# Pairing heads two apart so that a weight piece's rows are neighbours, loading queries ahead of keys, and a new order of the first four chunks

## The chip, the cores and the metric

The kernel runs on one core of a Trainium2 chip. The metric is device time in microseconds (us) for one execution: the median over the runs shown. A core has a matrix engine (TensorE, PE in the profile, with its weight loads as PEld), VectorE (DVE), ScalarE (ACT), GpSimd (POOL) and SyncE (SP). SP, ACT and POOL also issue transfers, which sixteen DMA engines carry out. SBUF is the memory of 128 partitions that the engines work on, PSUM the memory that TensorE writes.

## The reference

Inputs are q, k and v (4 batches, 8 heads, 768 positions, 64 values a head, float32) and two weight matrices of float64, 512 x 2048 and 2048 x 512, which reach the kernel as 64-bit words.

```python
# attention (retention): gamma differs from head to head
for t in range(S):
    state = gamma * state + outer(k[t], v[t])
    y[t] = scale * q[t] @ state
x = y.transpose(0, 2, 1, 3).reshape(B * S, H * D)      # 3072 x 512
# then a gated layer
h = x @ w_in                                           # 3072 x 2048
sp = softplus(h)
out = (h * erf(sp)) @ w_out                            # 3072 x 512
```

## The kernel before, in words

The sequence of each batch is cut into chunks of 128 positions, six to a batch, 24 in all; chunk j is `j % 6` of batch `j // 6`. Two neighbouring chunks make a group of 256 tokens, which is the unit of the gated layer (`GT = 256`, 12 groups).

Within a chunk the recurrence is done as matrix products: the keys and the scaled queries are transposed (`ret_transpose`, T), scores are their product (`ret_scores`, S_), VectorE masks them with a triangle into a tile `am` (`ret_mask`, M), and the output is masked scores times V plus queries times the running state (`ret_out`, O_). `ret_out` also forms the chunk's own keys-times-values sum, which `ret_add` (A) adds to the state. `scale_q` (Q_) and `scale_v` (V_) multiply queries and values by per-head powers of the decay, which stand in `kq_s`.

Heads are handled in pairs, because two heads of 64 values fill the 128 partitions: pair `u` holds heads `2u` and `2u+1`. The output goes into a tile `xT` (`XC`) whose 128 partitions times four column groups are the 512 input features of the layer. In the kernel before, partition half `r` and group `g` hold head `4r + g`, so a group joins features that lie 256 rows apart in `w_in`.

The weights `w_in` come in eight pieces of 256 columns (1 MB of 64-bit words each). `load_piece` loads a piece into a tile `raw`, in transfers of 64 partitions. VectorE and ScalarE then convert the words to float32 (`conversion`, lines 184 to 210: five VectorE operations and one on ScalarE), and pieces 0 to 3 are converted in two halves. The generator `weight_steps` emits one step of it at a time: `next(weight_steps)` emits one, and `need("in", n)` emits until feature tile n is ready. Finishing a piece releases its `raw` tile and issues the load of the piece four further on; after pieces 0 and 1 also q, k and v of chunks 4 and 5 are loaded.

The order of work in the first stage is written out by hand. Loads are all issued on SP's queue, in the order k and q of a chunk, then v of the chunk before, with the first weight piece near the end. The calls below `T(0, 0)` fix the order on each engine, and `keep_warm` puts matmuls on the identity between them. The work of an engine runs strictly in that order. When the chunks 0 to 3 are done, `hidden_of` multiplies feature tiles of the weights with groups 0 and 1 (PE line 591), sixteen feature tiles in turn. Each result is copied by ScalarE into a tile `h` and stored to `HID` in device memory by two transfers on POOL's queue (line 601). The tiles `h`, and the small `am` of later chunks, share a ring of six buffers (`b2`). At feature tile 1, `load_block_scales` puts further transfers on POOL's queue: the row scale `by_b` (line 328) and sixteen small transfers into `kq_b` (line 332). The work of chunks 4 and 5 is spread over feature tiles 5 to 13 by the table `during`; `states` (lines 513, 524) makes their masked scores and states.

After that come ten groups in which TensorE multiplies with weights split into three parts (`unit`, line 616) while the remaining chunks are prepared, and then the last stage, which applies softplus and erf and multiplies with `w_out` (`project`, line 801).

Each transfer has a completion semaphore. SP and POOL each take theirs from eight in turn, and a transfer waits for the one that used its semaphore eight transfers earlier on that queue.

Of the kernel before, what the change touches and what calls it, by code (L numbers as in the profile page):

```python
# [21 lines left out]
P = 128  # L22
C = 128
JPC = 4
GT = 256


PAIRS = (0, 2, 1, 3)

BELOW = 1023 - 127  # L30

# [10 lines left out]
def kernel(  # L42
# [51 lines left out]
    KNP, VP = {}, {}  # L94

    def of_chunk(x, j):

        b, c = divmod(j, NC)
        return x[b, :, c * C : (c + 1) * C, :].rearrange("h p d -> p h d")

    def load(j):

        kq = b4("kq", [2, H, D])
        KN[j], QN[j] = kq[:, 0], kq[:, 1]
        for to, src in ((KN[j], k), (QN[j], q)):
            nc.sync.dma_start(to, of_chunk(src, j))  # L106

    def load_values(j):
        if j % 2 == 0:
# [4 lines left out]
    def load_pair(j):  # L114

        b, c = divmod(j, NC)
        KNP[j] = b4("kn", [2, H, D])
        KB[j], QB[j] = (b4(name, [HP, 2 * C]) for name in ("kb", "qb"))
        for s, d in itertools.product(range(2), range(2)):
            part = slice((2 * s + d) * 32, (2 * s + d + 1) * 32)  # L120
            for to, src in ((KB[j], k), (QB[j], q)):
                for u in range(HP):
                    nc.sync.dma_start(
                        to[part, u].rearrange("p (a d) -> p a d", d=32),
                        src[b, 2 * u + s, c * C : (c + 2) * C, d * 32 : (d + 1) * 32].rearrange(
                            "(a p) d -> p a d", p=32
                        ),
                    )
                yield
        for i in range(2):  # L130
            load_values(j + i)
        for i in range(2):
            KN[j + i] = KNP[j][:, i]
            nc.sync.dma_start(KN[j + i], of_chunk(k, j + i))
        yield

# [22 lines left out]

    def load_quarter(i):  # L160
# [140 lines left out]
    unscale = 1.0 / math.sqrt(D)  # L301

    def query_scale(c):
        nc.vector.reciprocal(kq_s[:, c, 1], kq_s[:, c, 0])
# [15 lines left out]
    def other_scales():  # L320
        query_scale(slice(2, NC))
# [3 lines left out]
    by_b = const.tile([P, 2, HP], F32, name="by_b")  # L325

    def load_block_scales():
        nc.gpsimd.dma_start(by_b[:, 1], decay_s)
        for s, d in itertools.product(range(2), range(2)):
            part = slice((2 * s + d) * 32, (2 * s + d + 1) * 32)  # L330
            for u in range(HP):
                nc.gpsimd.dma_start(
                    kq_b[part, 0, u, 0],
                    decay_k[:, 2 * u + s : 2 * u + s + 1].rearrange("(a p) h -> p (a h)", p=32),
                )

    def block_scales():
# [46 lines left out]
    def ret_transpose(j, part=None, names=None):  # L384
        for i, (x, store) in enumerate(((KN[j], KT), (QN[j], QT))):
            if part not in (None, i):
                continue
            p = ps_o.tile([P, HP, C], F32, name=names[i]) if names else ret_psum(ps_h if i else ps_r)
            for u in range(HP):
                nc.tensor.transpose(  # L390
                    p[:, u, :], x[:, 2 * u : 2 * u + 2, :].rearrange("p h d -> p (h d)"), ident
                )
            if i == 0:
# [23 lines left out]
    def ret_out(j, between=None, state_last=False):  # L417
# [21 lines left out]
            between()  # L439
        for h in (0, 4, 1, 5, 2, 6, 3, 7):  # L440
            nc.tensor.matmul(
                place(h), V[j][:, h, :], AM[j][:, h % 2, h // 2, :],
                start=(not c and h % 4 < 2), stop=True, skip_group_check=True,
            )

        new = SU[j] = pp[0][:, 2:, :].rearrange("p a (b d) -> p (a b) d", d=D)
        for h in range(H):
            r = h % 2
            nc.tensor.matmul(
                new[r * D : (r + 1) * D, h // 2, :], KN[j][:, h, :], V[j][:, h, :],  # L450
                start=False, stop=True, skip_group_check=True,
            )
        for r in range(2):
# [37 lines left out]
    def begin(j, pool=ps_h):  # L491

        SC[j] = [ret_psum(pool) for _ in range(2)]
        for hp in range(HP):
            for a, s in itertools.product(range(2), range(2)):
                t, own = slice(a * D, (a + 1) * D), slice(s * D, (s + 1) * D)
                nc.tensor.matmul(  # L497
                    SC[j][s][t, hp, :D], KT[j][own, hp, t], QT[j][own, hp, t], start=True, stop=True,
                )
        for u in range(HP):  # L500
            for r in range(2):
                for a in additions(j):
                    t, h = slice(a * D, (a + 1) * D), 2 * u + r
                    nc.tensor.matmul(  # L504
                        SC[j][a][r * D : (r + 1) * D, u, D:], KN[j][t, h, :], V[j][t, h, :],
                        start=True, stop=True,
                    )

# [17 lines left out]
    def results(j, names=None, pool=ps_r):  # L526
# [20 lines left out]
        for crossed in range(2):  # L547
            for u in PAIRS:
                for a in range(2):
# [2 lines left out]
                    own = slice(col * D, (col + 1) * D)  # L552
                    nc.tensor.matmul(  # L553
                        pp[a][own, 2 + u % 2, :D] if crossed else pp[a][own, u % 2, t],
                        V[j][t, 2 * u + r, :],
                        AM[j][t, r, u],
                        start=False, stop=True, skip_group_check=True,
                    )
# [416 lines left out]
```

## Time and profile before

| | |
|---|---|
| runs | 627.85, 628.66, 631.52 us, median 628.66 |
| profiled execution | 630.29 us, span 628.6 us |
| TensorE busy | 617.5 us (98%) |
| VectorE, ScalarE, GpSimd busy | 472.9, 346.8, 99.8 us |
| granted TensorE clock | 0.999 |

The profile is one execution. "Span" is the time from the first to the last recorded instruction; the execution takes slightly longer. In rows of the timeline the first number is the start, the second the duration, and what stands in brackets is the idle time of the engine ahead of it and what ended that. SPq, POOLq and the like are an engine's queue of instructions. "L591" is line 591 of the kernel before. The DMA rows give mean rates over all sixteen DMA engines.

### The profile page before, as it was taken

What the parts mean: (1) busy time and instruction counts of PE and PEld (TensorE: products, weight loads), DVE (VectorE), ACT (ScalarE), POOL (GpSimd) and SP (SyncE); (2) the same over time, 40 slices, a digit from 0 to 9 for tenths busy, and PEclk for the clock granted to TensorE, in tenths of its full rate; (3) what the DMA queues carried; (4) which work ended last, traced back from release to release, by engine and by line L of the source; (5) the groups of instructions that cost most, each with busy time, mean ns of one, the idle gap of its engine ahead of it and who ended that gap; (6) DMA issues with size and microseconds to landing.
All of it is one profiled execution on the core that took longest, in us unless ns stands there. A gap on an engine that the chain in (4) does not pass through costs nothing.

```text
span 628.6 us, 14668 instructions
## 1 busy us (share of the span) xinstructions
PE 617.5 (98%) x6080; PEld 555.9 (88%) x6080; DVE 472.9 (75%) x608; ACT 346.8 (55%) x430; POOL 99.8 (16%) x189
## 2 busy tenths in 40 slices
PE   8899999999999999999999999999999999999997
PEld 7688789999999999999999978888888888888886
DVE  4887899849598887878777997867676686768650
ACT  3333353322323333232349779898889889888920
POOL 1054442222322413222111110000000000000000
PEclk9999999999999999999999999999999999999999
DMA  9999888986859898787945751453334314432300
GB/s 190 209 217 213 227 211 192 244 224 150 242 142 262 207 237 227 214 219 190 271 165 167 261 170 70 136 168 101 115 119 168 129 43 162 139 94 103 101 33 34
DMA packets 165426, 106.37 MB, mean 169 GB/s; under 512 B 139632, under 2 KB 143984, under 8 KB 165360
## 3 DMA queue, kind: packets, MB, share of 16 engines
q1 hardware_dynamic: 152608, 67.53, 44.4%
q0 software_dynamic: 12192, 37.77, 17.7%
q8 instruction: 47, 0.77, 0.5%
q10 hardware_dynamic: 560, 0.14, 0.1%
q14 instruction: 19, 0.16, 0.1%
HBM read 69.75 MB, written 35.65 MB: 168 GB/s over the span
## 4 chain that ended last, share of the span: by engine, by line
PE 89%; DMA 6%; SPq 2%; DVE 1%; issue 1%; POOL 1%; ACT 0%; DVEq 0%; POOLq 0%
PE o L616 35%; PE o L801 21%; PE hp L801 10%; PE r L801 10%; PE hp L591 4%; DMA hid<-h 3%; DMA kq_b<-decay_k_dram 2%; SPq L106 1%; DMA v<-in_v_dram 1%; PE hp L497 1%; PE hp L616 1%; PE r L616 1%; PE r L542 1%; DMA raw<-in_moe_w_in_dram 1%; PE hp L504 1%; PE r L553 1%
## 5 line engine op out<-in xcount | busy, mean ns | idle before, releaser
L616 PE MATMUL o<-x_hi,w_hi 128*128 128x256 f32 x600 | 149.6, 287 | 0.0
L616 PE MATMUL o<-x_lo,w_lo 128*128 128x256 f32 x600 | 147.2, 283 | 0.6 <-issue 0.6
L616 PEld LDWEIGHTS o<-x_hi,w_hi 128*128 128x128 f32 x600 | 115.0, 192 | 2.1 <-issue 0.7
L263 ACT ACTIVATE h<-o 128x512 f32<-128x512 f32 x75 | 44.7, 596 | 127.9 <-PE o L616 127.1
L616 PEld LDWEIGHTS o<-x_lo,w_lo 128*128 128x128 f32 x600 | 115.1, 192 | 0.1
L756 DVE TENSOR_TENSOR e<-hid,e 128x1024 f32<-128x1024 f32 x48 | 56.6, 1222 | 58.2 <-ACT e L746 58.2
L616 PE MATMUL o<-x_dif,w_dif 128*128 128x256 f32 x600 | 84.1, 283 | 0.0
L639 POOL DMA_DIRECT2D hid<-h x80 | 44.6, 558 | 206.7 <-DVE h L264 204.3
L616 PEld LDWEIGHTS o<-x_dif,w_dif 128*128 128x128 f32 x600 | 77.4, 192 | 0.0
L801 PE MATMUL o<-w_dif,g_dif 128*128 128x512 f32 x192 | 73.7, 389 | 0.0
L264 DVE SCALAR_TENSOR_TENSOR h<-o,h 128x512 f32<-128x512 f32 x75 | 51.2, 683 | 25.5 <-ACT h L263 13.1
L801 PE MATMUL o<-w_lo,g_lo 128*128 128x512 f32 x168 | 65.4, 389 | 0.0
L801 PE MATMUL o<-w_hi,g_hi 128*128 128x512 f32 x168 | 65.4, 389 | 0.0
L257 DVE SCALAR_TENSOR_TENSOR g_dif<-g_hi,g_lo 128x1024 fp32r<-128x1024 f32 x48 | 58.8, 1225 | 3.2
L255 ACT ACTIVATE g_hi<-e 128x1024 fp32r<-128x1024 f32 x48 | 51.0, 1063 | 17.8 <-DVE e L756 15.1
L256 DVE TENSOR_TENSOR g_lo<-e,g_hi 128x1024 fp32r<-128x1024 f32 x48 | 58.6, 1222 | 0.2
L591 PE MATMUL hp<-xT,w 128*128 128x256 f32 x256 | 56.9, 381 | 1.6 <-DVE w L210 1.6
L591 PEld LDWEIGHTS hp<-xT,w 128*128 128x128 f32 x256 | 48.1, 190 | 8.3 <-issue 1.2
L746 ACT ACTIVATE e<-e 128x1024 f32<-128x1024 f32 x48 | 48.2, 1053 | 0.3
L742 ACT ACTIVATE e<-hid 128x1024 f32<-128x1024 f32 x48 | 48.2, 1052 | 0.3
L801 PEld LDWEIGHTS o<-w_dif,g_dif 128*128 128x128 f32 x192 | 36.0, 188 | 7.5
L801 PE MATMUL hp<-w_dif,g_dif 128*128 128x512 f32 x96 | 37.5, 390 | 0.6 <-DVE h L264 0.6
(166 smaller groups left out, 1069.9 us busy)
## 6 DMA issues: line engine op xcount, KB each, us to landing
hid<-hid SPq DMA_DIRECT2D x48, 512.0 KB, 4.8
hid<-h POOLq DMA_DIRECT2D x80, 256.0 KB, 3.6
raw<-in_moe_w_out_dram POOLq DMA_DIRECT2D x32, 256.0 KB, 5.1
v<-in_v_dram SPq DMA_DIRECT2D x24, 256.0 KB, 5.7
out_dram<-y SPq DMA_DIRECT2D x23, 256.0 KB, 2.1
kb<-in_k_dram SPq DMA_DIRECT2D x144, 32.0 KB, 3.2
qb<-in_q_dram SPq DMA_DIRECT2D x144, 32.0 KB, 3.0
kn<-in_k_dram SPq DMA_DIRECT2D x18, 256.0 KB, 6.7
```

The costliest lines, as they stand in the source:

```text
L255: nc.scalar.activation(hi, x, AF.Copy, scale=KEEP)
L256: nc.vector.tensor_tensor(lo, x, hi.bitcast(F32), op=ALU.subtract)
L257: nc.vector.scalar_tensor_tensor(dif, hi.bitcast(F32), Z, lo.bitcast(F32), op0=ALU.mult, op1=ALU.subtract)
L263: nc.scalar.activation(to, a, AF.Copy, scale=1 + 1 / Z)
L264: nc.vector.scalar_tensor_tensor(to, b, -1 / Z, to, op0=ALU.mult, op1=ALU.add)
L591: nc.tensor.matmul(HP_[ft][:, g], w[:, kk, ft % 2 * P : (ft % 2 + 1) * P], XC[g][:, kk], start=(kk == 0), stop=(kk == n_k - 1),)
L616: nc.tensor.matmul(to[:, u], W[n][i][:, kk * 2 * P + u * P : kk * 2 * P + (u + 1) * P], X[g][i][:, kk], start=(u == 0 and kk == 0 and i == ...
L639: nc.gpsimd.dma_start(HID[g][:, 2 * n : 2 * n + 2], h)
L742: nc.scalar.activation(E[n], HID_[n], AF.Softplus)
L746: nc.scalar.activation(E[n], E[n], AF.Erf)
L756: nc.vector.tensor_tensor(E[n], HID_.pop(n), E[n], op=ALU.mult)
L801: nc.tensor.matmul(Y[g][t][x // 2], G[n][x][:, f, t * P : (t + 1) * P], W_OUT[ft // 2][x][:, ft % 2 * d_model : (ft % 2 + 1) * d_model], s ...
```

## The change

A function gives the new pairing, for all chunks:

```diff
+def head(u, r):
+    return u // 2 + u % 2 * 4 + 2 * r
```

So the pairs are heads (0, 2), (4, 6), (1, 3), (5, 7). Every place that used `2 * u + r` for a head of V, K or a scale now uses `head`. Partition half `r` and group `g` of `xT` now hold head `2g + r`, which is the order of the rows of `w_in`. The first six chunks hold their queries and keys in the order of the pairs in SBUF, which takes two transfers each:

```diff
-        for to, src in ((KN[j], k), (QN[j], q)):
-            nc.sync.dma_start(to, of_chunk(src, j))
+        for to, src in ((QN[j], q), (KN[j], k)):
+            for c in range(2):
+                nc.sync.dma_start(to[:, c * HP : (c + 1) * HP], of_chunk(src, j)[:, c::2])
+        SLOT[j] = lambda u, r: 2 * u + r
```

A weight piece is loaded by two transfers of 128 partitions (piece 0 by two for each half):

```diff
-    def load_piece(n, *parts):
+    def load_piece(n, part=None):
...
-        rows = (slice(2), slice(2, 4)) if n == 0 else (slice(4),)
-        for part, g, r in itertools.product(parts or (None,), rows, range(2)):
-            f = slice(2 * P) if part is None else slice(part * P, (part + 1) * P)
+        f = slice(2 * P) if part is None else slice(part * P, (part + 1) * P)
+        for g in range(0, n_k, 2):
             nc.sync.dma_start(
-                RAW[n][r * D : (r + 1) * D].rearrange("p (g f) -> p g f", g=n_k)[:, g, f],
-                w_in[r * DH : (r + 1) * DH, n * 2 * P : (n + 1) * 2 * P].rearrange(
-                    "(g p) f -> p g f", p=D
-                )[:, g, f],
+                RAW[n].rearrange("p (g f) -> p g f", g=n_k)[:, g : g + 2, f],
+                w_in[g * P : (g + 2) * P, n * 2 * P : (n + 1) * 2 * P].rearrange(
+                    "(g p) f -> p g f", p=P
+                )[:, :, f],
             )
```

The order of the loads at the start:

```diff
     for j in range(1, JPC):
         load(j)
-        load_values(j - 1)
+        if j < JPC - 1:
+            load_values(j - 1)
     load_piece(0, 0)
+    load_values(JPC - 2)
+    load_piece(0, 1)
     load_values(JPC - 1)
-    load_piece(0, 1)
     for n in range(1, 4):
-        load_piece(n, 0, 1)
+        load_piece(n)
```

The row scale of later chunks follows the new pairs, in four transfers instead of one:

```diff
-        nc.gpsimd.dma_start(by_b[:, 1], decay_s)
+        for s, i in itertools.product(range(2), range(2)):
+            nc.gpsimd.dma_start(
+                by_b[s * D : (s + 1) * D, 1, 2 * i : 2 * i + 2], decay_s[i * D : (i + 1) * D, s::2]
+            )
```

`query_scale` writes its reciprocal in the order of the pairs. The order of the first four chunks, written out anew:

```diff
-    T(0, 0)
-    keep_warm(2)
     Q_(0)
     second_scales()
     T(0, 1)
-    keep_warm(1)
+    T(0, 0)
+    keep_warm(2)
+    Q_(1)
+    other_scales()
+    S_(0)
+    T(1, 1)
     T(1, 0)
-    S_(0)
-    Q_(1)
-    T(1, 1)
     keep_warm(2)
-    other_scales()
     M(0)
-    V_(0)
     S_(1)
     Q_(2)
+    V_(0)
+    T(2, 1)
+    T(2, 0)
     O_(0)
-    T(2, 0)
     M(1)
+    V_(1)
+    S_(2)
+    Q_(3)
     A(0)
-    T(2, 1)
-    V_(1)
-    Q_(3)
-
-    def next_scores():
-        S_(2)
-        M(2)
-
-    O_(1, next_scores)
-    T(3, 0)
+    M(2)
+    T(3, 1)
+    next(weight_steps)
+    O_(1, lambda: T(3, 0))
+    next(weight_steps)
     V_(2)
     A(1)
-    T(3, 1)
     need("in", 0)
+    S_(3)
     O_(2)
-    S_(3)
+    next(weight_steps)
+    M(3)
+    A(2)
     V_(3)
     next(weight_steps)
-    A(2)
-    M(3)
+    ret_out(JPC - 1, lambda: hidden_of(0, 0), state_last=True)
     need("in", 1)
-    ret_out(JPC - 1, lambda: hidden_of(0, 0), state_last=True)
     hidden_of(1, 0)
```

So the first three VectorE operations on weight piece 0 come ahead of the values of chunk 2, the last two behind them.

More of the change, by code (lines that the diff above doesn't have):

```diff
@@ L93 @@
     KN, QN, V, KB, QB, KT, QT, SC, AM, SU = {}, {}, {}, {}, {}, {}, {}, {}, {}, {}
-    KNP, VP = {}, {}
+    KNP, VP, SLOT = {}, {}, {}
     def of_chunk(x, j):
@@ L132, in load_pair @@
         for i in range(2):
-            KN[j + i] = KNP[j][:, i]
+            KN[j + i], SLOT[j + i] = KNP[j][:, i], head
             nc.sync.dma_start(KN[j + i], of_chunk(k, j + i))
@@ L303, in query_scale @@
     def query_scale(c):
-        nc.vector.reciprocal(kq_s[:, c, 1], kq_s[:, c, 0])
+        c = slice(c, c + 1) if isinstance(c, int) else c
+        nc.vector.reciprocal(
+            kq_s[:, c, 1].rearrange("p n (c g) -> p n c g", c=2),
+            kq_s[:, c, 0].rearrange("p n (g c) -> p n c g", c=2),
+        )
         nc.vector.tensor_scalar(kq_s[:, c, 1], kq_s[:, c, 1], unscale, None, op0=ALU.mult)
@@ L333, in load_block_scales @@
                     kq_b[part, 0, u, 0],
-                    decay_k[:, 2 * u + s : 2 * u + s + 1].rearrange("(a p) h -> p (a h)", p=32),
+                    decay_k[:, head(u, s) : head(u, s) + 1].rearrange("(a p) h -> p (a h)", p=32),
                 )
@@ L392, in ret_transpose @@
                 )
-            if i == 0:
+            if j not in KT:
                 KQT = b4("kqT", [2, HP, C])
@@ L441, in ret_out @@
             nc.tensor.matmul(
-                place(h), V[j][:, h, :], AM[j][:, h % 2, h // 2, :],
+                place(h), V[j][:, head(h // 2, h % 2), :], AM[j][:, h % 2, h // 2, :],
                 start=(not c and h % 4 < 2), stop=True, skip_group_check=True,
@@ L449, in ret_out @@
             nc.tensor.matmul(
-                new[r * D : (r + 1) * D, h // 2, :], KN[j][:, h, :], V[j][:, h, :],
+                new[r * D : (r + 1) * D, h // 2, :],
+                KN[j][:, SLOT[j](h // 2, r), :], V[j][:, head(h // 2, r), :],
                 start=False, stop=True, skip_group_check=True,
@@ L554, in results @@
                         pp[a][own, 2 + u % 2, :D] if crossed else pp[a][own, u % 2, t],
-                        V[j][t, 2 * u + r, :],
+                        V[j][t, head(u, r), :],
                         AM[j][t, r, u],
```

7 lines of the change are left out of this document (4 added, 3 removed).

## The prediction

> **What bounds the kernel now.** I began with the page's first two parts, to see which engine is full.
>
> ```profile
> span 628.6 us, 14668 instructions
> PE 617.5 (98%) x6080; PEld 555.9 (88%) x6080; DVE 472.9 (75%) x608; ACT 346.8 (55%) x430; POOL 99.8 (16%) x189
> PE   8899999999999999999999999999999999999997
> ```
>
> TensorE is busy 617.5 of 628.6 us: all waits together are 11.1 us, so no reordering can gain much over that, and only where it touches the waits. The view by windows (the first numbers are the length and PE's busy time) says where they lie.
>
> ```profile
> 0.00:30.00 30.00, 25.01 (x308) 21.58 (x309) 19.20 (x42) 10.20 (x21) 2.45 (x15) 1.00 1.02 198
> 30.00:60.00 30.00, 30.00 (x202) 26.27 (x202) 24.26 (x39) 11.55 (x19) 16.71 (x29) 1.00 1.12 212
> 60.00:70.00 10.00, 8.88 (x104) 7.59 (x104) 7.60 (x11) 3.55 (x7) 4.06 (x9) 1.00 1.08 317
> 70.00:130.00 60.00, 60.00 (x826) 56.09 (x825) 53.69 (x76) 22.97 (x36) 19.51 (x37) 1.00 0.85 201
> 130.00:365.00 235.00, 233.85 (x3501) 229.62 (x3500) 188.13 (x280) 94.21 (x151) 55.69 (x99) 1.00 0.78 212
> 365.00:628.60 263.60, 259.79 (x1147) 214.76 (x1145) 180.02 (x165) 204.30 (x199) 1.39 (x3) 1.00 0.33 110
> ```
>
> PE idles 4.99 us in the first 30 us, 1.12 in 60 to 70, and 4.96 after 130, in stages that the change does not reorder. From 30 to 60 and from 70 to 130 it never stops. So the change can act on two places: the moment from which PE is continuously busy, and the hole between 60 and 70. The waits of PE and the chain up to 70 us name them.
>
> ```profile
> PE hp L591 <- DVE w L210: 1.6, 2, 1.1
> PE o L434 <- DVE state L459: 1.4, 1, 1.4
> PE o L542 <- DVE state L524: 1.1, 1, 1.1
> ...
> 11.62 7.25 DMA v<-in_v_dram
> 19.52 4.97 DMA raw<-in_moe_w_in_dram
> 29.10 3.71 PE hp L591 x16
> 33.72 8.86 DMA hid<-h
> 45.65 9.58 DMA kq_b<-decay_k_dram
> 56.28 8.28 DMA hid<-h
> 64.69 0.76 DVE am L513 x2
> ```
>
> The chain (start, duration) runs on loads to 24.5 us: v of chunk 2, then the second half of weight piece 0. At 29.10 the stream of hidden matmuls starts and holds PE. Later, a score mask waits until 64.56 for a store of h. The mask's tile is the ninth in a ring of six that it shares with h, so it takes the buffer of the third h. That store was late because POOL's queue was.
>
> VectorE in order of time shows the first stage in detail:
>
> ```profile
> 5.96 0.69 DVE L376 TENSOR_TENSOR kq<-kq,kq_s 128x512 f32<-128x512 f32 x1 [2.70 <-DMA kq<-in_q_dram]
> ...
> 15.58 0.69 DVE L376 TENSOR_TENSOR kq<-kq,kq_s 128x512 f32<-128x512 f32 x1 [0.80 <-DMA kq<-in_q_dram]
> ...
> 18.89 0.69 DVE L376 TENSOR_TENSOR v<-v,kq_s 128x512 f32<-128x512 f32 x1 [1.42 <-DMA v<-in_v_dram]
> ...
> 20.71 0.43 DVE L184 TENSOR_SCALAR power<-raw 128x512 uint32<-128x512 uint32 x1 [0.79 <-DMA raw<-in_moe_w_in_dram]
> 21.05 0.42 DVE L191 TENSOR_SCALAR w<-raw 128x512 uint32<-128x512 uint32 x1
> 21.50 0.70 DVE L196 SCALAR_TENSOR_TENSOR w<-w,raw 128x512 f32<-128x512 uint32 x1
> 22.11 0.69 DVE L198 SCALAR_TENSOR_TENSOR power<-raw,power 128x512 uint32<-128x512 uint32 x1
> ...
> 24.61 0.43 DVE L184 TENSOR_SCALAR power<-raw 128x512 uint32<-128x512 uint32 x1 [0.48 <-DMA raw<-in_moe_w_in_dram]
> ...
> 28.26 0.69 DVE L210 SCALAR_TENSOR_TENSOR w<-w,power 128x512 f32<-128x512 f32 x1
> ```
>
> From v of chunk 2 (18.89) to the end of the second half-piece (28.95) are 10.06 us, VectorE idle in them only 0.79 + 0.48 = 1.27, both times for raw.
>
> **The change, part by part.** *Weight pieces.* The DMA view over three stretches gives the rates.
>
> ```profile
> DMA packets 8709, 2.21 MB, mean 221 GB/s; under 512 B 8708, under 2 KB 8708, under 8 KB 8708
> ...
> DMA packets 2271, 2.19 MB, mean 219 GB/s; under 512 B 130, under 2 KB 2270, under 8 KB 2271
> ...
> DMA packets 3604, 3.77 MB, mean 315 GB/s; under 512 B 2382, under 2 KB 2382, under 8 KB 3601
> ```
>
> The first is 5 to 15 us, q, k and v in 256 B packets; the second 26 to 36 us, raw alone in 1 KB packets, every DMA on 64 partitions; the third 60 to 72 us, mixed traffic, much of it to and from 128 partitions. Packets four times as large as those of q and k, yet no more than 219 GB/s: something about the 64-partition form holds them down. No row shows a raw load on 128 partitions; its bounds are 219 GB/s (nothing gained) and 315, and I take 315, since its form is that of the third stretch. A half piece (524 KB) then takes 1.66 us instead of 2.39.
>
> The Trainium skill, "SBUF — State Buffer", section "Door 1: The DMA port swizzle", says that 64 neighbouring partitions reach 8 of 16 ports, at most about 218 GB/s, against 328 measured for 1 MiB on 128 partitions. The 219 above agrees; by its 328 a half piece would take 1.60 us and the sum below would gain 0.06 us more.
>
> *Order of loads.* Ten pieces of 256 KB (q and k of four chunks, v of two) stay ahead of everything, now with q before k. The first half of raw 0 goes ahead of v of chunk 2, the second ahead of v of chunk 3. The tenth piece landed at 15.58 (above); the pace of 256 B packets does not change, so k of chunk 3 lands there now. The half piece lands at 15.58 + 1.66 = 17.2, v of chunk 2 at 17.2 + 256 KB / 221 GB/s (1.19) = 18.4, the second half at 20.1, v of chunk 3 at 21.3. On VectorE the first three operations of the first half (0.34 + 0.45 + 0.61 = 1.40 from start to start) now stand ahead of that v: 17.2 + 1.4 = 18.6. At 219 GB/s the half would land at 18.0 and v at 19.2, so 18.0 + 1.4 = 19.4. In the trace v of chunk 2 landed at 18.89 instead of 15.58 + 1.19 = 16.8, 2.1 late; if it straggles so again, 18.4 + 2.1 = 20.5, and I go on to 21.3 with the slow rate. I take 18.9, between 18.6 and 19.4.
>
> From there the same VectorE work remains, without the three operations (1.40) and without the two idle times (1.27), because the second half landed at 20.1 and is wanted some 2.3 us after 18.9: 10.06 − 1.40 − 1.27 = 7.39. The second half-piece ends at 26.3, PE starts its stream 0.15 later, as now (28.95 to 29.10), at 26.45: **2.65 us saved**, ends 2.95 (from 18.6) and 0.25 (from 21.3).
>
> *q ahead of k, other order of the four chunks, fewer warming matmuls.* Transposes and scores of chunk 0 come out some tenths earlier, because q's scaling no longer follows the second arrival, but PE and VectorE then wait for later chunks as the rows at 5.96 and 15.58 show: nothing, hidden by the loads. If that cover were gone, scaling and transposing q, about 1.3 us a chunk, would be bared. The scale's reciprocal in another order and the head numbers in V's and K's slices move the same bytes: nothing.
>
> *Halved q and k loads.* 24 DMAs instead of 12, each taking a turn among SP's eight completion semaphores, so eight halves of 128 KB (1 MB, 4.7 us at 221 GB/s) are in flight at most. SP's issue costs at least
>
> ```profile
> 0.81 0.44 SPq L106 DMA_DIRECT2D kq<-in_k_dram  x1
> ```
>
> per DMA before the queue pushes back; two of them, 0.88, are below the 1.19 us that the data take: nothing, as long as loads set the pace; bared, 0.44 us for each of eight extra issues, 3.5 us. Raw's issues fall from 28 to 18.
>
> *POOL's queue.* The row scale `by_b` becomes four DMAs instead of one, so the queue holds 22 ahead of the second h's stores where it held 19. Eight may be outstanding:
>
> ```profile
> 35.51 3.16 POOL L332 DMA_DIRECT2D kq_b<-decay_k_dram  x5
> 42.86 4.42 POOL L332 DMA_DIRECT2D kq_b<-decay_k_dram  x8 [4.19 <-DMA hid<-h]
> ...
> DMA to landing us min/median/max: 6.0/7.5/9.6
> ...
> hid<-h POOLq DMA_DIRECT2D x4, 128.0 KB, 3.3
> ```
>
> The third row is of the kq_b loads, the last of 72 to 80 us, where the DMA engines are half idle. The third h's last store was the 23rd DMA of this queue and becomes the 26th: it waits for three landings one behind the other now, its own included (8.86, 9.58, 8.28), and for four then. Behind it stand the mask, VectorE's whole queue, and PE. With today's latencies: first store at 33.72 − 2.65 = 31.07, its pair 0.63 later, + 8.86 + 7.5 + 7.5 + 8.28 = 63.8. To cost no wait it must land at 64.56 − 1.12 − 2.65 = 60.8. So the stall would be 3.0 instead of 1.1, a loss of **1.9**. But latencies average 8.0 there because the engines are full (DMA share 1.12 in 30 to 60); 7.3 is enough to lose the stall. Of the 6.4 MB moved in those 30 us (212 GB/s) about 4.2 are raw pieces 4 to 7: at 315 GB/s they need 13.3 us and the rest 10, so nearly a quarter of the time comes free; between 8.0 and the 3.3 of the idle stretch that makes 8.0 × 0.77 + 3.3 × 0.23 = 6.9. I take the stall as gone, **1.1 us saved**; ends 1.1 saved and 1.9 lost.
>
> **Sum.** 2.65 + 1.1 = 3.75 us. The profiled execution took 630.29 us, 1.69 beyond its span: 626.5. The median of the runs shown is 1.63 lower: 628.66 − 3.75 = **624.9 us**. Runs before lay between 627.85 and 631.52. A measurement tells about 1% (6.3 us) from no change here.
>
> **Rivals.**
> (a) *The start is gained, the stall stays* because `by_b`'s three DMAs eat what the emptier engines give: −2.65 ± 0.5, 626.0. For it: the needed latency (7.3) and my estimate (6.9) are close. Against: raw leaves the engines earlier.
> (b) *Slower: POOL's queue decides.* Latency stays at 8.0, four landings in a row, and v of chunk 2 straggles to 21.3, so that the start gains 0.25: +1.9 − 0.25, 630.3. It decides once the mean latency there exceeds 7.3 us and the start gains under 1.9. For it: no kq_b load landed in under 6.0 us, and q, k and v of chunks 4 and 5 cross that stretch as before; against: it needs both.
> (c) *The change doesn't do what it says*: raw on 128 partitions still flows at 219 GB/s. VectorE takes v of chunk 2 at 19.4, and the second half (19.2 + 2.39 = 21.6) is there when it is wanted, so the start gains 2.15 by the new order alone; the full engines leave the stall at 3.0: −2.15 + 1.9, 628.4. For it: nothing on 128 partitions with such packets is in the trace; against: the 315.
> (d) *PE stays slow longer.* Its first matmuls take nearly twice as long, which four transposes show:
>
> ```profile
> 1.47 3.35 PE L354 MATMUL o<-ident 128*128 128x128 f32 x14 [1.47 <-POOL ident masks.py:199]
> 4.61 1.06 PE L390 MATMUL r<-ident,kq 128*128 128x128 f32 x4
> ...
> 7.42 0.60 PE L390 MATMUL r<-ident,kq 128*128 128x128 f32 x4
> ```
>
> PE now idles between the warming matmuls (done at 4.8) and q's transposes: q lands one piece earlier than at 5.96, at 4.8, and is scaled by 5.5. If that keeps PE slow for another 6 us, 3 us of work take 6, of which 1.4 vanish in today's wait for v of chunk 2 (state L459 above): −3.75 + 1.6, 626.5. The Trainium skill, "TensorE: Matmul & The Clock Gate", section "What's actually happening", has PE at full speed after a busy window of about 3.4 us and slow again after an idle one. By that rule 0.7 us need not cost anything, and no idle time as long as its window is expected here.
>
> **How the numbers follow.** Forecast 0.50, (a) 0.20, (b) 0.12, (c) 0.13, (d) 0.05. The forecast's own ends are 2.95 + 1.1 saved (624.6) and 0.25 + 1.1 (627.3); the range goes down to 622.0 for the spread of runs and a start limited only by bytes, and up to 630.3 for (b). All cases lie within 1%; past it the gain would need all of the first hole and the second (4.99 + 1.12 us) with a kind run, 0.14; a loss of 6.3 us needs a transfer that becomes much slower than any row shows, 0.08.
>
> **What would show it.** Right: raw rates near 315 GB/s between 20 and 32 us; hidden matmuls continuous from about 26.5; VectorE without idle time from v of chunk 2 on; PE's 60 to 70 window full; kq_b landing below 7 us. Wrong: raw still at 219, v of chunk 2 landing after 20.5, a wait of the mask for h's store above 1 us, or SP issuing halves one by one behind their semaphores before 16 us.

## The result, and the profile after

The changed kernel takes 626.34 us (median of six runs, 626.11 to 626.62). The kernel before, measured beside it, takes 629.10 us (627.85 to 631.52). The ratio is 0.9953, with a 95% interval of 0.9934 to 0.9971. The gain of 2.8 us is thus real, but it is half a per cent. The forecast of 624.9 was 1.4 us too low. The time lies inside the range.

The profiled execution after took 626.11 us with a span of 624.4, so profile against profile the gain is 630.29 − 626.11 = 4.2 us. That this is more than the medians give becomes important below.

First the view by windows of the kernel after, with the same columns as before (length, busy time of PE, PEld, DVE, ACT and POOL, then PE's granted clock, the DMA share and GB/s).

```profile
0.00:30.00 30.00, 27.26 (x316) 23.85 (x317) 20.84 (x44) 10.53 (x21) 2.46 (x15) 1.00 1.03 271
30.00:60.00 30.00, 30.00 (x203) 26.27 (x202) 26.76 (x43) 12.72 (x19) 21.42 (x37) 1.00 1.00 256
60.00:70.00 10.00, 10.00 (x152) 8.51 (x151) 9.06 (x15) 4.20 (x8) 1.90 (x5) 1.00 0.50 113
130.00:365.00 235.00, 234.41 (x3491) 229.51 (x3490) 189.67 (x278) 97.89 (x154) 55.16 (x98) 1.00 0.76 211
365.00:624.40 259.40, 255.72 (x1129) 211.40 (x1127) 176.04 (x161) 200.33 (x195) 0.54 (x1) 1.00 0.33 108
```

PE's idle time in the first 30 us fell from 4.99 to 2.74 us (2.25 gained). The 1.12 us between 60 and 70 are gone. From 130 to 365 it fell from 1.15 to 0.59, in a stage that the change does not reorder. From 365 on it fell from 3.81 to 3.68. These four make 4.06 of the 4.2 us: 3.37 in the two places that the prediction named, 0.69 after 130.

The waits of PE (engine, line, what was waited for: us in total, times, longest) no longer list the state that stood behind the late mask:

```profile
PE o L372 <- POOL ident masks.py:199: 1.5, 1, 1.5
PE hp L408 <- DVE kq L394: 0.9, 1, 0.9
PE hp L818 <- DVE h L273: 0.6, 1, 0.6
PE r L420 <- ACT kqT L414: 0.3, 1, 0.3
```

The chain up to 80 us (start, duration) shows what now sets the start of the stream:

```profile
12.95 5.01 DMA raw<-in_moe_w_in_dram
18.05 0.44 DVE power L193
18.52 0.73 ACT power L196
19.24 0.48 ACT kqT L414
19.77 0.37 PE r L420
...
27.05 22.66 PE hp L610 x104
```

Before, the chain went through v of chunk 2 and the second half of the weight piece. Now it goes through the first half, which lands at 17.96. ScalarE's exponent waits for it, the copy of chunk 3's transposes stands behind the exponent, and the scores behind the copy. From 19.77 PE has no pause. VectorE's side ends at nearly the same time, from the same landing:

```profile
18.05 0.43 DVE L193 TENSOR_SCALAR power<-raw 128x512 uint32<-128x512 uint32 x1 [0.30 <-DMA raw<-in_moe_w_in_dram]
...
19.46 0.69 DVE L394 TENSOR_TENSOR v<-v,kq_s 128x512 f32<-128x512 f32 x1
...
26.19 0.69 DVE L219 SCALAR_TENSOR_TENSOR w<-w,power 128x512 f32<-128x512 f32 x1
```

From v of chunk 2 to the end of the second half-piece are 26.88 − 19.46 = 7.42 us. The stream starts at 27.05 instead of 29.10.

The DMA view of 20 to 28 us gives the rate of raw on 128 partitions, and POOL's rows from 30 to 60, with the landing times of the small loads (median, last row), give its queue:

```profile
DMA packets 1635, 3.04 MB, mean 380 GB/s; under 512 B 167, under 2 KB 167, under 8 KB 1634
...
31.65 1.27 POOL L620 DMA_DIRECT2D hid<-h  x2 [24.43 <-ACT h L618]
32.91 2.46 POOL L344 DMA_DIRECT2D by_b<-decay_s_dram  x4
...
43.69 4.36 POOL L350 DMA_DIRECT2D kq_b<-decay_k_dram  x7 [0.84 <-DMA kq_b<-decay_k_dram]
...
kq_b<-decay_k_dram POOLq DMA_DIRECT2D x16, 0.5 KB, 6.0
```

Raw moves at 380 GB/s where it had 219. POOL waits for a landing at most 0.84 us at a time there, where it had waited 4.19, and the small loads land after 6.0 us instead of 7.5.

### The profile page after: what moved, and what is told of

Same layout as the page of the kernel before. It is cut to its first block, busy times and chain, and to the rows that moved or that the text cites. A ratio compares the mean times of both kernels' runs of the same rounds, so it can differ in the third digit from the quotient of the medians.

```text
span 624.4 us, 14678 instructions
## 1 busy us (share of the span) xinstructions
PE 617.4 (99%) x6078; PEld 556.2 (89%) x6078; DVE 473.3 (76%) x608; ACT 347.2 (56%) x430; POOL 101.6 (16%) x192
## 4 chain that ended last, share of the span: by engine, by line
PE 96%; SPq 2%; DMA 1%; issue 0%; DVE 0%; ACT 0%; DVEq 0%
PE o L635 35%; PE o L818 21%; PE hp L818 10%; PE r L818 10%; PE hp L610 9%; SPq L115 2%; PE hp L516 1%; PE hp L635 1%; PE r L635 1%; PE r L561 1%; DMA raw<-in_moe_w_in_dram 1%; PE r L516 1%; PE hp L523 1%; PE r L572 1%; PE r L523 1%; PE hp L561 1%
```

## The experiments

**1. The changed kernel with raw in its old 64-partition transfers, everything else as changed.** This separates the form of the loads from the new order.

```diff
-        for g in range(0, n_k, 2):
-            nc.sync.dma_start(
-                RAW[n].rearrange("p (g f) -> p g f", g=n_k)[:, g : g + 2, f],
...
+        for g in (slice(2), slice(2, 4)) if n == 0 else (slice(4),):
+            for r in range(2):
+                own = slice(r * D, (r + 1) * D)
+                nc.sync.dma_start(
+                    RAW[n][own].rearrange("p (g f) -> p g f", g=n_k)[:, g, f],
...
```

> The changed kernel, with each weight piece again loaded in transfers of 64 partitions (same tile layout, same order of loads, same four-chunk order). Theory (the 128-partition form carries the gain): raw flows at about 219 GB/s again between 20 and 36 us, the first half piece lands some 0.7 us later than the 17.96 us of the changed kernel, the hidden stream starts near 27.8 instead of 27.05, the DMA engines stay full to 60 us, POOL's four landings in a row cost a wait of the mask of 2 to 3 us: span 627 to 628.5 against 624.4. Rival (the order alone carries it): stream start by 27.2 and no wait of the mask, span 624.4 to 625.0.

Measured: 632.48 us (median of 10), beside 629.06 of the kernel before; ratio 1.0055 (1.0027 to 1.0084). Without the 128-partition form the change loses 3.4 us; the form is worth 632.48 − 626.3 = 6.1 us here. The windows (60 to 80 us), PE's waits, the chain behind the wait, and the DMA view of 20 to 36 us show where:

```profile
60.00:80.00 20.00, 17.93 (x180) 15.28 (x179) 16.98 (x28) 7.12 (x12) 8.97 (x17) 0.91 0.84 226
...
PE o L563 <- DVE state L545: 2.1, 1, 2.1
...
66.50 1.57 PE o L410 x8
68.07 4.59 PE hp L612 x16
...
DMA packets 2723, 3.48 MB, mean 218 GB/s; under 512 B 1127, under 2 KB 1184, under 8 KB 2722
```

Raw is back at 218 GB/s, the stream starts at 27.92 (0.87 later than with the form), the hole is there with 2.1 us, and behind it PE runs slowly: the same 16 hidden matmuls take 4.59 us where the kernel after needs 3.46, and the 8 transposes 1.57 instead of 1.02. That is 1.68 us in which PE counts as busy, with a granted clock of 0.91 in the window. 0.87 + 2.07 + 1.68 = 4.6 of the 5.6 us by which the spans differ (630.0 against 624.4); the remaining 1.0 I have not placed.

**2. Pairing and 128-partition loads kept, with the old order of loads and chunks and keys ahead of queries.**

```diff
-        for to, src in ((QN[j], q), (KN[j], k)):
+        for to, src in ((KN[j], k), (QN[j], q)):
...
-        if j < JPC - 1:
-            load_values(j - 1)
+        load_values(j - 1)
     load_piece(0, 0)
-    load_values(JPC - 2)
+    load_values(JPC - 1)
     load_piece(0, 1)
-    load_values(JPC - 1)
```

The four chunks' steps are in the old order as well, as in the kernel before; q and k stay in halves.

> The changed kernel with the pairing and the 128-partition weight loads kept, but keys ahead of queries, the old order of the loads and the old four-chunk order. Theory (the weight loads carry the gain, the order little): v of chunk 2 no longer has 64-partition raw behind it, so it lands near 16.8 to 17.5 instead of 18.9, the first half piece near 18.5, stream start 26.5 to 27.3, PE at full speed from 6.5 us as before, no wait of the mask: span 624.0 to 624.8. Rival (the new order is needed): stream start at 28 or later, span 625.4 or more.

Measured: 626.23 us (5 runs), ratio 0.9955 (0.9941 to 0.9969), span 624.5, start of the stream 27.27. This is the time of the changed kernel (626.34) within its spread. The two orders carry nothing that can be measured. The start comes about at the same moment by another chain, though: it runs through q of chunk 3, which VectorE takes at 16.68, and VectorE never waits for raw behind it.

**3. Two more warming matmuls, so that PE does not idle ahead of the first transposes.** This is for the rival in which PE stays slow longer.

```diff
-    keep_warm(7)
+    keep_warm(9)
```

> The changed kernel with nine warming matmuls instead of seven ahead of the first transposes, so that PE does not idle between 4.8 and 5.75 us. Theory (that idle time delayed PE's switch to full speed from about 6.5 to 9 us, but the stream start hangs on the landing of raw and VectorE's 7.4 us after it): the switch comes near 6.5, transposes and scores of chunk 0 about 1.5 us earlier, stream start earlier by at most 0.3, span 624.0 to 624.5. Rival (the start is bound by PE's slow phase): stream start 1 us or more earlier, span 623.4 or less.

Measured: 626.18 us (4 runs), ratio 0.9954 (0.9937 to 0.9972). First four rows of PE after (the last of them at full pace), then the first row at that pace here, and then VectorE here:

```profile
5.75 1.12 PE L408 MATMUL hp<-ident,kq 128*128 128x128 f32 x4 [0.92 <-DVE kq L394]
6.65 1.06 PE L408 MATMUL r<-ident,kq 128*128 128x128 f32 x4
7.51 1.06 PE L372 MATMUL o<-ident 128*128 128x128 f32 x4
...
10.35 0.60 PE L408 MATMUL r<-ident,kq 128*128 128x128 f32 x4
```

```profile
6.30 0.60 PE L408 MATMUL r<-ident,kq 128*128 128x128 f32 x4
...
18.40 0.43 DVE L193 TENSOR_SCALAR power<-raw 128x512 uint32<-128x512 uint32 x1 [1.78 <-DMA raw<-in_moe_w_in_dram]
```

The rival's mechanism did occur: in the kernel after, four transposes still take 1.06 us at 7.5, behind a pause of 0.92 us. With nine warming matmuls they take 0.60 already at 6.30, and the first mask comes 1.1 us earlier (8.82 against 9.95). Nothing of that reaches the end: VectorE then waits 1.78 us instead of 0.30 for raw, and the stream starts at 27.39, 8.99 us behind VectorE's first operation on raw (9.00 in the kernel after). In these two executions the slow phase is hidden behind the load; run 11 has one in which it is not.

**4. The kernel before with `by_b` in four transfers.** One edit alone, on POOL's queue.

```diff
-        nc.gpsimd.dma_start(by_b[:, 1], decay_s)
+        for i in range(4):
+            nc.gpsimd.dma_start(by_b[i * 32 : (i + 1) * 32, 1], decay_s[i * 32 : (i + 1) * 32])
```

> The kernel before, with the row scale by_b loaded by four transfers of 32 partitions instead of one, so that the third h's last store is the 26th of POOL's queue instead of the 23rd. Theory (four landings in a row instead of three, at latencies of 7 to 9 us): the mask's wait on PE grows from 1.1 to about 3 us, span 630 to 631 against 628.6. Rival (the queue has slack, the wait had another cause): span within 0.4 us of 628.6, wait unchanged.

Measured: 635.48 us (4 runs), ratio 1.0106 (1.0086 to 1.0127): 6.4 us slower. The windows (60 to 80 us), the waits and the chain:

```profile
60.00:80.00 20.00, 15.29 (x168) 12.55 (x167) 13.35 (x22) 7.56 (x12) 6.50 (x12) 0.91 0.80 222
...
PE hp L592 <- ACT h L600: 4.7, 1, 4.7
...
63.39 0.54 POOL L602 DMA_DIRECT2D hid<-h  x1 [2.64 <-DMA hid<-h]
...
55.59 9.09 DMA hid<-h
...
65.42 5.41 PE hp L592 x16
```

The store that lands at 64.68 is one of the second h, which POOL issues from 55.03 on instead of from 51.97. The eighth h takes its buffer, and ScalarE's copy waits for it:

```profile
64.78 0.58 ACT L600 COPY h<-hp 128x512 f32<-128x512 f32 x1 [11.10 <-DMA hid<-h]
```

PE waits 4.7 us for that copy. (In the profile of before the same copy waited 4.37 us, until 58.24, and PE did not stop.) Then the 16 matmuls take 5.41 instead of 3.46 us. So three small transfers more on POOL's queue cost the hole 4.7 − 1.1 = 3.6 us and another 1.95 us of slow matmuls. Beside one execution's span (628.6) the span is 4.5 longer, beside that of run 5 (627.1) 6.0. The lane was really there, and its price was three times the 1.9 us of the prediction. It was also another wait than the expected one: three landings in a row, as before, end in a store that is wanted earlier, not four in the store for which the mask waits.

**5. The kernel before, unchanged, for a second profile.**

> The kernel before, unchanged, profiled a second time: its runs spread over 3.7 us, those of the changed kernel over 0.5. Theory (what varies is the wait for POOL's stores, between 60 and 70 us, with PE's slow phase behind a long one): the span less the idle time of PE in 60 to 70 us stays near 627.5, whatever the span. Rival (it varies in the first 30 us or after 130): the idle time in 60 to 70 stays 1.1 while the span differs by 1 us or more.

Measured: 628.97 us (10 runs); the profiled execution took 628.83, its span is 627.1.

```profile
0.00:30.00 30.00, 25.41 (x310) 22.26 (x311) 19.88 (x42) 10.58 (x21) 2.45 (x15) 1.00 1.07 204
60.00:80.00 20.00, 19.55 (x253) 16.40 (x252) 18.35 (x29) 9.35 (x16) 9.34 (x18) 1.00 0.78 219
130.00:365.00 235.00, 234.43 (x3501) 229.90 (x3500) 188.56 (x279) 95.73 (x152) 55.89 (x99) 1.00 0.78 213
```

This execution is 1.5 us shorter than the one that the prediction read. The idle time is 0.40 smaller in the first 30 us, 0.67 smaller between 60 and 80 (0.45 instead of 1.12), and 0.58 smaller from 130 to 365: together 1.65, of which PE's busy time, 0.2 longer, takes a little back. The stall is thus not a constant of the kernel: it was 1.1 in one execution and 0.5 in another. The theory put down for this run, that only the stall varies, does not hold: 0.98 of the 1.65 lie elsewhere. The stall has two ways in, too. Here it is again the eighth h that waits for a store of the second,

```profile
59.71 0.58 ACT L599 COPY h<-hp 128x512 f32<-128x512 f32 x1 [6.27 <-DMA hid<-h]
```

and behind that copy stand an exponent on ScalarE, then VectorE's conversion, then the mask at 63.79.

**6. The kernel before with the small scale transfers earlier on POOL, right behind the other scales; no h is stored at that time.**

```diff
+    load_block_scales()
...
-        1: [(load_block_scales,)],
```

> The kernel before, with the seventeen small transfers of by_b and kq_b issued on POOL at the start of the four chunks instead of at feature tile 1, so that stores of h find POOL's queue empty. Theory (the queue is the cause of the wait): PE idles under 0.2 us in 60 to 80 us, stream start 29.1 to 29.6, span 627.3 to 628.0, runs within 1 us of each other. Rival (full DMA engines make the stores late by themselves): a wait of 0.8 us or more remains and the runs spread over 2 us or more.

Measured: 630.07 us (10 runs) beside 628.66; ratio 1.002 (1.0005 to 1.0035).

```profile
0.00:30.00 30.00, 24.58 (x304) 21.22 (x304) 17.97 (x38) 9.74 (x20) 11.81 (x32) 0.94 1.14 199
...
60.00:80.00 20.00, 20.00 (x242) 17.12 (x244) 18.86 (x30) 6.65 (x12) 6.62 (x13) 1.00 0.83 195
```

The window from 60 to 80 is full: the stall comes from those transfers standing in POOL's queue at that time. But the stream starts at 30.36, 1.3 us later than in the prediction's profile. From 5 to 15 us the loads now get 205 GB/s instead of 221, and PE waits 1.8 us for a state, behind which the clock is lower (0.94). The cure costs as much as the stall.

**7. Both: 64-partition raw (kernel of run 1) with the early scale transfers.** It uses the edits of runs 1 and 6.

> The changed kernel with weight pieces in transfers of 64 partitions, as in the first experiment (span 630.0), and with the small transfers of by_b and kq_b issued on POOL at the start of the four chunks. Theory (of the 5.6 us that the 64-partition form cost, 0.9 are the later start and the rest is the wait behind POOL's queue with the slow PE after it): span 625.2 to 626.0, no idle PE in 60 to 80. Rival (slow raw starves the stream by itself): span 627.5 or more.

Measured: 630.49 us (10 runs), ratio 1.0026 (1.001 to 1.0042). The window from 60 to 80 is full (20.00), although raw moves as slowly as before. The stream starts at 30.64, 2.7 us later than in run 1, behind a wait of 2.7 us for raw and at a granted clock of 0.94 in the first 30 us; that is why the span (628.5) is not the 625.2 to 626.0 that the theory expected. So slow raw alone doesn't open the hole; it needs POOL's queue as well. Beside run 1 (632.48, with 629.06 for the kernel before, here 628.66) the earlier transfers gain some 1.6 us in spite of the later start.

**8. The changed kernel with nine warming matmuls, early scale transfers, and raw's first half ahead of the keys of chunk 3.** An attempt to take the load off the chain.

```diff
+            if j == JPC - 1 and src is k:
+                load_piece(0, 0)
...
-    load_piece(0, 0)
...
-    keep_warm(7)
+    keep_warm(9)
...
+    load_block_scales()
...
-    O_(1, lambda: T(3, 0))
+    O_(1)
+    T(3, 0)
...
-        1: [(load_block_scales,)],
```

> The changed kernel with nine warming matmuls, the small transfers of by_b and kq_b early on POOL, and the first half of weight piece 0 loaded ahead of the keys of chunk 3, whose transposes come behind the output of chunk 1. Theory (the stream start hangs on the landing of that half, 17.96 us in the changed kernel): it lands near 16.7, VectorE goes through without its wait, v of chunk 2 (landing near 18.8) becomes the bound, stream start 26.3 to 26.8, span 623.8 to 624.3. Rival (PE's own work from chunk 3 on sets the start, since the transposes come later): stream start 27.2 or later, span 624.5 or more.

Measured: 627.25 us (12 runs) beside 628.66, ratio 0.9962 (0.9945 to 0.9979), start 27.94: slower than the changed kernel, where the theory expected a gain. VectorE had raw at 17.14 without waiting, but then

```profile
20.58 0.69 DVE L395 TENSOR_TENSOR v<-v,kq_s 128x512 f32<-128x512 f32 x1 [1.96 <-DMA v<-in_v_dram]
```

it waited for v of chunk 2, which came 1.1 us later than in the kernel after (19.46). What is pulled ahead pushes something else back, and all of it is wanted before the stream. The 20 small transfers took their share too (215 GB/s from 5 to 15 us, 224 after).

**9. The changed kernel again**, beside runs 10 to 12.

> The changed kernel, unchanged, profiled a second time beside the next three. Theory (without a wait for POOL's stores nothing is left that varies): span within 0.5 us of 624.4, stream start 26.8 to 27.4, no idle PE from 30 to 130. Rival (its steadiness was chance): a wait of 0.5 us or more between 60 and 80 us.

Measured: 626.22 us (5 runs, 625.86 to 626.62) beside 629.13, ratio 0.9948 (0.9928 to 0.9968), span 624.4: the same as the first time.

**10. The kernel before with q and k in two transfers a chunk.** Halving alone.

```diff
-            nc.sync.dma_start(to, of_chunk(src, j))
+            for c in range(2):
+                nc.sync.dma_start(to[:, c * HP : (c + 1) * HP], of_chunk(src, j)[:, c * HP : (c + 1) * HP])
```

> The kernel before, with the loads of q and k of the first six chunks halved by heads, as the change does, and nothing else. Prediction as on record (nothing, the loads set the pace): stream start 28.7 to 29.1 and span less the idle time of 60 to 80 us at 626.6 to 627.5, as in the two profiles of the kernel before. Rival (SP waits for the oldest of eight semaphores and issues later: ten pieces took SP 11.6 us in the changed kernel, 10.8 before): q of chunk 3 lands 0.5 us or more later than 15.58 and the start comes 0.4 to 1.0 us later.

Measured: 629.92 us (10 runs), ratio 1.001 (0.9994 to 1.0025): no difference that can be told. VectorE's row for q of chunk 3, the tenth piece, shows a cost all the same:

```profile
16.82 0.69 DVE L377 TENSOR_TENSOR kq<-kq,kq_s 128x512 f32<-128x512 f32 x1 [2.15 <-DMA kq<-in_q_dram]
```

In one piece it is there at 15.58 in the prediction's profile, at 15.19 in run 5 and at 15.15 in run 4. In halves it comes at 16.82 here and at 16.68 in run 2, although the rate from 5 to 15 us is the same (222 GB/s) and q of chunk 2 comes as before (11.82, against 11.96). SP issues the last half by 11.97, 0.4 later than the whole piece by 11.57. The stream starts at 28.79, as in run 5 (28.71): the late piece costs the start nothing here.

Halving by itself is not the reason that it is late, because in the changed kernel the tenth piece, also in halves, lands at 15.4 (15.2 in run 9). In each of these traces one transfer of the stretch from 15 to 19 us lands 1 to 2 us later than the pace of those ahead of it would give. In the kernel before it is v of chunk 2 (18.89, and 18.39 in run 5), here and in run 2 the last half of q, in the changed kernel the first half of raw. What delays it is not shown.

**11. The changed kernel with `by_b`'s four transfers from ScalarE's queue** instead of POOL's.

```diff
-            nc.gpsimd.dma_start(
+            nc.scalar.dma_start(
```

> The changed kernel with the four transfers of by_b issued by ScalarE instead of POOL, so that the third h's last store is the 22nd of POOL's queue instead of the 26th. Theory (with weight pieces on 128 partitions POOL's queue has slack): span 624.2 to 624.8, no change. Rival (the queue still costs something further on): span 624.0 or less.

Measured: 626.44 us (6 runs), ratio 0.9952 (0.9936 to 0.9968). The first store of the second h is issued at 44.33 instead of 48.03, 3.7 us earlier, and nothing is gained by it: PE has no wait in 60 to 80 with or without these four transfers on POOL. The rival in which the stall stays because of `by_b` has no ground: with faster raw there is slack.

The profiled execution has a span of 625.2, more than the 624.8 expected, and a start at 27.64. The edit is hardly the reason, since `by_b` is issued only behind 30 us. VectorE's first mask and its first operation on raw show what is:

```profile
10.49 0.69 DVE L431 TENSOR_TENSOR am<-r,causal 128x512 f32<-128x512 f32 x1 [2.28 <-PE hp L420]
...
18.40 0.42 DVE L193 TENSOR_SCALAR power<-raw 128x512 uint32<-128x512 uint32 x1
```

Raw's first half landed at 16.9 this time, and VectorE, coming late from the masks, did not wait for it. PE's slow first matmuls lasted to about 11 us instead of 9, and the chain to the stream runs through them. So the slow phase is not always hidden: here it set the start, 0.6 us later than in the kernel after.

**12. The changed kernel with nine warming matmuls and the first weight step behind chunk 3's transposes**, so that ScalarE's copy no longer stands behind the exponent.

```diff
-    keep_warm(7)
+    keep_warm(9)
...
-    next(weight_steps)
-    O_(1, lambda: T(3, 0))
+    O_(1, lambda: (T(3, 0), next(weight_steps)))
```

> The changed kernel with nine warming matmuls, and with the first step on weight piece 0 emitted behind the transposes of chunk 3's keys, so that ScalarE copies them ahead of the exponent that waits for raw. Theory (VectorE's work from the landing of raw on, 7.4 us behind 1.4, and PE's work from the scores of chunk 3 on end within 0.2 us of each other, so freeing PE alone gives little): stream start 26.7 to 27.2, span 624.0 to 624.5. Rival (PE's chain alone is the bound): start under 26.5, span 623.8 or less.

Measured: 625.96 us (5 runs, 625.62 to 626.35), ratio 0.9942 (0.9919 to 0.9964). The stream starts at 27.25, not earlier:

```profile
18.49 0.43 DVE L193 TENSOR_SCALAR power<-raw 128x512 uint32<-128x512 uint32 x1 [1.37 <-DMA raw<-in_moe_w_in_dram]
```

Raw landed 0.44 us later in this execution (18.40). From VectorE's first operation on it to the stream are 8.76 us instead of 9.00; the path now runs over v of chunk 2 and the state to PE's outputs, no longer over ScalarE's exponent. So the edit shortened the chain by 0.24 us, and the later landing took that back. It is the lowest median of all, below both kernels, but only 0.3 us under the changed kernel beside it (626.22), with overlapping runs: a real difference between these two is not shown.

## Why the prediction was near, and where it was off

**The mechanism held.** Most of the time (3.37 of the profiles' 4.2 us) was gained in the two places that it named, by the terms that it named for them. Without the 128-partition form the change loses (run 1), with it the old orders give the same time (run 2), so neither of the new orders carries anything that can be measured.

**Start term: 2.65 forecast, 2.05 measured** (29.10 to 27.05 in the profiles). The failed step is "A half piece (524 KB) then takes 1.66 us instead of 2.39", for the first half of piece 0. What lands ahead of it came as forecast: k of chunk 3, the tenth piece, at 15.4 instead of 15.58. The DMA view of the kernel after gives the time from issue to landing for the last half of that k and the two transfers of raw's first half, which are issued at 11.61, 12.37 and 12.95:

```profile
kq<-in_k_dram SPq DMA_DIRECT2D x1, 128.0 KB, 3.8
...
raw<-in_moe_w_in_dram SPq DMA_DIRECT2D x1, 256.0 KB, 3.8
...
raw<-in_moe_w_in_dram SPq DMA_DIRECT2D x1, 256.0 KB, 5.0
```

The first transfer lands 0.8 us behind k, the second 1.8 us behind the first. The half took some 2.5 us, a little longer than at the old rate (2.39), and landed at 17.96 instead of 17.2. The prediction had read such a straggler in the trace of before (v of chunk 2, 2.1 us late), but priced it for v alone; this time it fell on raw. Why one transfer straggles stays open (run 10). Later, between 20 and 28 us, raw runs at 380 GB/s, faster than the 315 taken, but nobody waits for the second half, so this gains nothing at the start. The other half of the working fits: v of chunk 2 was bound by VectorE's three operations behind that half, at 19.46 (18.05 + 1.40), and the remaining VectorE work, forecast at 7.39, took 7.42. 19.46 is a little beyond the 19.4 which the prediction had given as its slow end.

**Stall term: 1.1 forecast, 1.12 measured in the profiles** (0.45 where run 5 is the profile of before). The reason given, that the small loads land sooner when raw leaves the engines earlier, shows as 6.0 us instead of 7.5 (forecast 6.9, needed 7.3). Run 1 is the counter-test: with raw at 218 GB/s and POOL's queue as changed, the hole is 2.1 us.

**The sum against the profiled execution: 3.75 forecast, 4.2 measured.** That these agree so well is in part luck: the start fell 0.6 short, and 0.7 came from the stages after 130 us, of which the forecast had nothing. The sum gave 626.5 for a kernel like that execution's, and the profiled execution after took 626.11.

**What failed is the step from there to the median**: "The median of the runs shown is 1.63 lower: 628.66 − 3.75 = 624.9". It assumed that what the profiled execution of before had above its median would also stand above the median of after. Run 5 shows that this excess was itself idle time of PE, 0.40 at the start, 0.67 in the stall and 0.58 after 130 us. The first two lie in the places that the change empties, so they were subtracted twice: as part of the 3.75, and again in the 1.63. The kernel after has hardly any of it: six runs within 0.5 us, where six of before spread over 3.7. Against run 5's execution the change gains 1.66 at the start (28.71 to 27.05) and 0.45 in the hole, 2.1 of the 2.7 between the spans; the medians differ by 2.8. The 626.5 of the sum was the better forecast.

**The rivals.** (a), the start gained and the stall kept, did not happen; run 11 shows no sign of it. (b), POOL's queue decides, did not happen either, yet its mechanism is the strongest effect in this study. Its price was worked out as a later landing of the third h's store alone. Run 4 shows that the second h's store can be the one that is missed, and runs 1 and 4 show a second part, the matmuls slowed behind the wait (1.7 and 1.95 us). With it and with raw at the old rate the kernel would have been slower by 3.4 us, as run 1 is. (c), raw still at 219 GB/s, would by its working have given 628.4; run 1, which has raw at that rate (on 64 partitions), took 632.5: it gained 1.2 us at the start (29.10 to 27.92) instead of 2.15, and behind its stall stood the slow matmuls, which the working lacked. (d), PE slow for longer, happened as described, but not at its price: it was hidden behind raw in the kernel after (run 3), and in run 11's execution, where raw was early, the start came 0.6 us later, not 1.6.

## What to carry to other kernels

Before adding transfers to a queue, however small, count what stands behind them, how many landings in a row they add, and which of the stores behind them is wanted first: three more transfers, of 0.5 KB, cost 6.4 us where nothing was to spare (run 4), and nothing where the engines drained faster (run 11). Forecast the new median from a typical execution of before, or say which of the profiled execution's waits the change removes, and don't subtract the offset to the median a second time for them. Where all loads of a start are wanted before the stream, putting one ahead only moves the wait: shorten the transfers themselves.

## What the runs showed of the hardware

Raw moves at 219 GB/s (before) and 218 GB/s (run 1) when each transfer covers 64 partitions, and at 380 GB/s on 128 (after). The Trainium skill, "SBUF — State Buffer", section "Door 1: The DMA port swizzle", gives about 218 for the one, which agrees, and for the other 328 at 1 MiB and 436 as the limit; over the 3.04 MB of eight microseconds here the measured rate lies between these two.

A wait of PE can cost more than its length. Behind waits of 2.1 us (run 1) and 4.7 us (run 4) matmuls ran slower, at a granted clock of 0.91 over the window of 20 us and of 0.50 from 67 to 70 us in run 1 and from 66 to 68 us in run 4. How long the wait is does not settle it. Behind one of 1.93 us, earlier in run 1, the matmuls kept their pace; behind one of 1.82 us in run 6 they did not:

```profile
20.64 0.37 PE L422 MATMUL r<-kqT 64*128 64x128 f32 x1 [1.93 <-ACT kqT L416]
...
20.85 0.27 PE L422 MATMUL r<-kqT 64*128 64x128 f32 x1
```

```profile
20.16 0.67 PE L434 MATMUL o<-kqT,state 64*64 64x128 f32 x16 [1.82 <-DVE state L459]
...
21.76 1.08 PE L449 MATMUL o<-v,kq 128*64 128x64 f32 x16
```

The same sixteen matmuls take 0.64 us at 16.69 in that run, and the granted clock from 22 to 24 us is 0.50. The Trainium skill, "TensorE: Matmul & The Clock Gate", section "What's actually happening", has PE throttled again after an idle window of about 3.4 us. The wait of 4.7 us in run 4 agrees; those of 2.1 and 1.8 us were shorter and throttled PE all the same. What decides it below 3.4 us is not shown.

At the start the rows of run 3 and of after show the other side: with a pause of 0.92 us behind the first matmuls full pace comes at about 9 us instead of 6.3, with the granted clock of the first 30 us listed as 1.00 in both, so that there the slow phase is seen in the rows' durations alone.

The profiles before, after and of runs 2, 5, 9 and 10 have one more thing in common around the transfer that straggles (run 10): a single packet of the instruction queue, which starts between 13.4 and 15.2 us. In the kernel after the DMA view of 13 to 21 us lists it as

```profile
q8 instruction: 1, 0.02, 0.8%
```

0.8% of 16 engines over 8 us is about 1 us of one engine, which is about what the straggler of that kernel lacks. That this packet holds up the loads on its engine is a guess; no run moved it.
